# A token product split into full matmuls and 64-row tiles, moved into another burst and other banks, with the additions behind the squares

## The chip, the cores and the metric

The kernel runs on one core of a Trainium2 chip. The metric is the device time of one execution in microseconds. Each kernel was run several times, together with the kernel before on the same chip; a profile of one execution of each is read alongside. The engines' names in the profile: PE is TensorE (PEld its weight loads), ACT is ScalarE, DVE is VectorE, POOL is GpSimd, and SP is SyncE, which here only issues DMAs. The granted clock is the share of TensorE's full clock that the profile's records show.

## The reference, cut to what matters

```python
scores = scale * np.matmul(q, k.transpose(0, 1, 3, 2))       # 8 batches, 12 heads, 448 tokens, width 64
attn = np.maximum(scores, 0.0) ** 2 / S
x = (attn @ v)                                               # put together to (8, 448, 768)
h = np.maximum(xt @ w_tok1, 0.0) @ w_tok2                    # xt: tokens last; 448 -> 256 -> 448
u = x + h.transpose(0, 2, 1)                                 # the residual addition
out = u + np.maximum(u @ w_ch1, 0.0) @ w_ch2                 # 768 -> 1536 -> 768
```

The product over tokens has a sum of 448 terms: three blocks of 128 tokens and one of 64. That last block of 64 is what the change is about.

## The kernel before

Work is cut into 24 groups of four heads. Step i of the main loop does the scores of group i, and the values, the transposition, the two token products and the residual addition of group i - 1. Between them stand units of the channel products of earlier batches, taken from a queue by `fill`: a unit of the first channel product is 6 matmuls, one of the second is 12. They are ballast that keeps TensorE busy while other engines work.

```python
def values(i, cs):                       # 7 x 4 tiles of 64x64, two banks, r = bank
    ...
        accs[i] = [ps_acc.tile([128, 512], FP32, tag=f"acc{r}", name="acc_ps") for r in range(2)]
    ...

def values_out(i, split=False):          # VectorE: bank r -> xT, scaled, 448 of 512 columns; the rest is zero
    ...

def token1(i):                           # full matmuls, the fourth block half zeros
    x_sb = x_tiles.pop(i)
    ps = ps_mm.tile([128, JC, 256], FP32, tag="bank", name="t1_ps")
    for j in range(JC):
        for c in range(4):
            nc.tensor.matmul(ps[:, j, :], lhsT=wt1[:, c, j * 128 : (j + 1) * 128],
                             rhs=x_sb[:, :, c, :], start=(c == 0), stop=(c == 3))
    r1 = mix.tile([128, JC, 256], BF16, name="r1_sb")
    nc.scalar.activation(r1, ps, AF.Relu)

def token2(i, ...):                      # h: 4 matmuls into acc0, acc1; then one VectorE addition per bank
    ...

for i in range(DB + 1, ND + 2):          # DB = 3, ND = 24, XDMA = 8
    ...
    scores(i, 0); scores(i, 1)
    values(i - 1, range(QC)); values_out(i - 1)
    scores(i, 2)
    ...
    x_back(i - 1)                        # from step 9 on a transposing DMA: xT -> x_sb
    ...
    square()                             # VectorE squares what scores left
    if i - 1 >= XDMA:
        fill(1 / 3)
    scores(i, 3); scores(i, 4)
    transposes(i + 1)                    # into acc0, acc1
    square()
    if not slow:                         # slow: steps up to 6
        fill(2 / 9)
    token1(i - 1)
    fill(1 / 3 if slow else 1 / 9, least=1)
    scores(i, 5); scores(i, 6)
    token2(i - 1)
    ...
    square()
    fill(1 / 3, least=1 if slow else 0)
```

(Written shorter: lines joined, conditions at the loop's ends cut.) The two banks named acc0 and acc1 go round: values, transposes, h, values again.

## Time and profile before

| | before |
|---|---|
| time, median of 6 runs | 377.62 us (377.41 to 378.09) |
| span of the profile | 375.6 us |
| PE busy | 365.1 us, 97% |
| DVE, ACT busy | 208.1 us (55%), 211.4 us (56%) |
| PE waits named by the profile, together | some 6 us, of which 5 in the first 40 us |

How to read it: busy shares of the engines beside PE say nothing as long as what they deliver comes before PE asks for it. So the question at each spot is which arrives last: the turn of a matmul in PE's stream, or the bank and the data that it needs.

Two lines of groups show the token product before. Columns: line, engine, operation, out<-in, shapes, count, then busy us, mean ns of one, and the idle time ahead with what ended it.

```profile
L261 PE MATMUL t_ps<-x_sb,wt 128*128 128x256 bf16 x192 | 24.9, 273 | 1.8 <-DMA x_sb<-xT 0.8 <-DVE qkT L156 0.5 <-DVE x_sb L252 0.5
...
L269 ACT ACTIVATE r_sb<-t_ps 128x512 bf16<-128x512 f32 x24 | 14.3, 597 | 20.8 <-PE t_ps L261 20.8
```

Eight matmuls and one activation per group of heads. The 0.8 us wait is the one in step 9.

### The profile page before, as it was taken

What the parts mean: (1) busy time and instruction counts of PE and PEld (TensorE: products, weight loads), DVE (VectorE), ACT (ScalarE), POOL (GpSimd) and SP (SyncE); (2) the same over time, 40 slices, a digit from 0 to 9 for tenths busy, and PEclk for the clock granted to TensorE, in tenths of its full rate; (3) what the DMA queues carried; (4) which work ended last, traced back from release to release, by engine and by line L of the source; (5) the groups of instructions that cost most, each with busy time, mean ns of one, the idle gap of its engine ahead of it and who ended that gap; (6) DMA issues with size and microseconds to landing.
All of it is one profiled execution on the core that took longest, in us unless ns stands there. A gap on an engine that the chain in (4) does not pass through costs nothing.

```text
span 375.6 us, 10084 instructions
## 1 busy us (share of the span) xinstructions
PE 365.1 (97%) x4335; PEld 200.8 (53%) x4335; DVE 208.1 (55%) x376; ACT 211.4 (56%) x295; POOL 100.7 (27%) x186
## 2 busy tenths in 40 slices
PE   8889999999999999999999999999999999999995
PEld 3444555555555555565555555555555654555563
DVE  2896688675567665466555575465555664221021
ACT  4887888777434457744675447754576346412400
POOL 8874548313230321430321303312300000000000
PEclk9999999999999999999999999999999999999999
DMA  8999999934987876756844897838550443433023
GB/s 153 112 142 203 173 205 185 191 46 70 133 155 171 164 148 110 91 94 129 151 71 65 148 151 125 125 62 159 111 95 12 92 101 85 58 70 86 0 62 107
DMA packets 69325, 43.30 MB, mean 115 GB/s; under 512 B 43360, under 2 KB 65824, under 8 KB 69280
## 3 DMA queue, kind: packets, MB, share of 16 engines
q0 software_dynamic: 24416, 21.47, 40.4%
q1 hardware_dynamic: 44560, 20.75, 25.3%
q8 instruction: 34, 0.56, 0.6%
q10 hardware_dynamic: 304, 0.43, 0.4%
q14 instruction: 11, 0.09, 0.1%
HBM read 43.38 MB, written 11.01 MB: 145 GB/s over the span
## 4 chain that ended last, share of the span: by engine, by line
PE 90%; DVE 5%; ACT 2%; DMA 1%; issue 0%; ACTq 0%
PE m_ps L335 29%; PE m_ps L374 29%; PE sc_ps L166 9%; PE acc_ps L199 8%; PE t_ps L261 5%; PE h_ps L284 5%; PE qkT_ps L142 2%; DVE at L187 2%; ACT at L180 2%; DMA x_sb<-xT 1%; PE warm_ps L437 1%; DVE uT_sb L294 1%; DVE qkT L156 1%; PE x_ps L243 1%; PE m_ps L353 1%; DVE x_sb L252 1%
## 5 line engine op out<-in xcount | busy, mean ns | idle before, releaser
L180 ACT ACTIVATE at<-sc_ps 128x896 bf16<-128x896 f32 x167 | 143.9, 921 | 59.2 <-PE sc_ps L166 59.2
L335 PE MATMUL m_ps<-uT_sb,wc 128*128 128x448 bf16 x564 | 115.6, 353 | 0.2 <-DVE uT_sb L294 0.2
L374 PE MATMUL m_ps<-wc,r_sb 128*128 128x384 bf16 x672 | 115.2, 326 | 0.0
L187 DVE TENSOR_TENSOR at<-at 128x896 bf16<-128x896 bf16 x168 | 97.6, 624 | 4.6 <-ACT at L180 4.6
L374 PEld LDWEIGHTS <-r_sb 128*128 128x128 bf16 x672 | 64.3, 98 | 45.6 <-issue 3.9
L342 ACT ACTIVATE r_sb<-m_ps 128x448 bf16<-128x448 f32 x94 | 51.2, 544 | 59.8 <-PE m_ps L335 59.5
L335 PEld LDWEIGHTS <-wc 128*128 128x128 bf16 x564 | 53.3, 98 | 49.8 <-issue 4.3
L381 DVE TENSOR_TENSOR out_sb<-m_ps,u_sb 128x384 f32<-128x384 f32 x56 | 31.1, 556 | 60.3 <-PE m_ps L374 59.3
L166 PE MATMUL sc_ps<-qkT 64*64 64x448 bf16 x672 | 52.8, 360 | 0.9 <-ACT at L180 0.5
L294 DVE TENSOR_TENSOR uT_sb<-h_ps,xT 128x448 bf16<-128x448 f32 x48 | 27.9, 620 | 38.7 <-PE h_ps L284 38.6
L217 DVE TENSOR_SCALAR xT<-acc_ps 128x448 bf16<-128x448 f32 x45 | 26.1, 620 | 34.8 <-PE acc_ps L199 34.8
L199 PE MATMUL acc_ps<-at,v_raw 64*64 64x448 bf16 x672 | 38.4, 350 | 0.6 <-ACT x_sb L252 0.5
L556 POOL COPY gate<-x_sb 1x1 bf16<-1x1 bf16 x12 | 2.2, 184 | 125.5 <-DMA x_sb<-xT 125.5
L83 POOL DMA_DIRECT2D q_raw<-in_q_dram x48 | 29.0, 615 | 20.4 <-DMA wc<-in_moe_w_ch_dram 16.5
L156 DVE COPY qkT<-qkT_ps 128x896 bf16<-128x896 bf16 x45 | 26.0, 619 | 14.6 <-PE qkT_ps L142 14.6
L83 POOL DMA_DIRECT2D v_raw<-in_v_dram x48 | 29.5, 639 | 7.6 <-DMA wc<-in_moe_w_ch_dram 4.7
L166 PEld LDWEIGHTS <-qkT 64*64 64x64 bf16 x672 | 15.6, 105 | 28.1 <-issue 23.8
L83 POOL DMA_DIRECT2D k_raw<-in_k_dram x46 | 28.1, 633 | 0.0
L199 PEld LDWEIGHTS <-v_raw 64*64 64x64 bf16 x672 | 20.3, 107 | 13.1 <-issue 1.7
L261 PE MATMUL t_ps<-x_sb,wt 128*128 128x256 bf16 x192 | 24.9, 273 | 1.8 <-DMA x_sb<-xT 0.8
L269 ACT ACTIVATE r_sb<-t_ps 128x512 bf16<-128x512 f32 x24 | 14.3, 597 | 20.8 <-PE t_ps L261 20.8
L284 PE MATMUL h_ps<-wt,r_sb 128*128 128x448 bf16 x96 | 22.5, 355 | 0.0
(41 smaller groups left out, 119.8 us busy)
## 6 DMA issues: line engine op xcount, KB each, us to landing
out_dram<-out_sb SPq DMA_DIRECT2D x54, 192.0 KB, 3.5
q_raw<-in_q_dram POOLq DMA_DIRECT2D x48, 112.0 KB, 4.3
v_raw<-in_v_dram POOLq DMA_DIRECT2D x48, 112.0 KB, 5.6
k_raw<-in_k_dram POOLq DMA_DIRECT2D x46, 112.0 KB, 5.7
wc<-in_moe_w_ch_dram POOLq DMA_DIRECT2D x4, 1152.0 KB, 10.7
u_sb<-uT_sb SPq DMA_TRANSPOSE x48, 2.6
x_sb<-xT SPq DMA_TRANSPOSE x16, 3.3
k_first<-in_k_dram SPq DMA_DIRECT2D x1, 224.0 KB, 3.5
```

The lines of the kernel that those rows point to most:

```text
L83: eng.dma_start(out=dst[64 * r : 64 * (r + 1)].rearrange("p g c d -> p g (c d)"), in_=src[b, h0 : h0 + 2].rearrange("g (p c) d -> p g (c d ...
L166: nc.tensor.matmul(ps[64 * r : 64 * (r + 1), g, :S], lhsT=sb[h, r, 1, c * 64 : (c + 1) * 64], rhs=sb[h, r, 0, :], start=True, stop=True, s ...
L180: nc.scalar.activation(at, ps[:, :, :S], AF.Relu)
L187: nc.vector.tensor_tensor(out=at, in0=at, in1=at, op=ALU.mult)
L199: nc.tensor.matmul(ps[r][64 * g : 64 * (g + 1), :S], lhsT=v_raw[h, g, c, :], rhs=at[h, g, :], start=(c == 0), stop=(c == QC - 1), skip_gro ...
L261: nc.tensor.matmul(ps[:, j, :], lhsT=wt1[:, c, j * 128 : (j + 1) * 128], rhs=x_sb[:, :, c, :], start=(c == 0), stop=(c == 3),)
L284: nc.tensor.matmul(parts[r][:, :S], lhsT=r1[:, j, r * 128 : (r + 1) * 128], rhs=wt2[:, j, :], start=(j == 0), stop=(j == JC - 1),)
L294: nc.vector.tensor_tensor(out=uT_tiles[b // 2][:, 2 * d + r, off : off + S], in0=parts[r][:, :S], in1=xT[b % 2][:, 2 * d + r, :S], op=ALU.add,
L335: nc.tensor.matmul(ps[:, :S], lhsT=wc1[:, g, e * 128 : (e + 1) * 128], rhs=uT[:, g, off : off + S], start=(g == 0), stop=(g == CC - 1),)
L342: nc.scalar.activation(r2[:, e, off : off + S], ps[:, :S], AF.Relu)
L374: nc.tensor.matmul(ps[:, :HN], lhsT=r2[:, e, t * 128 : (t + 1) * 128], rhs=wc2[:, e, cols], start=(e == 0), stop=(e == EC - 1),)
L381: nc.vector.tensor_tensor(out=o[:, cols].rearrange("n (g d) -> n g d", d=128), in0=ps[:, :HN].rearrange("n (g d) -> n g d", d=128), in1=u_ ...
```

## The change

Its intent: of the eight token matmuls, the two with the last 64 tokens use half the rows of the array for zeros. Now the last 64 tokens are written twice, side by side, so that after the transposition they lie on both row halves; the two row halves then work for the two output blocks (j) at once, as four tiles of 64 rows by 64 columns. They stand directly ahead of scores 5 and 6, which also are 64-row tiles, so that the tiling need not be changed for them alone; and the product goes into acc0 and acc1, one row half to each bank. Some fill goes ahead of it, and one unit now stands between scores 6 and h. Squares go ahead of the residual additions from step 7 on. In step 0 four warm-up matmuls go.

```diff
-            fill(1 / 3)
+            fill(0.37, least=1)
         ... scores 3, 4, transposes, square
-        if not slow:
-            fill(2 / 9)
-        if 0 <= i - 1 < ND:
-            token1(i - 1)
-        fill(1 / 3 if slow else 1 / 9, least=1)
+        if slow:
+            token1(i - 1)
+            fill(1 / 3, least=1)
+        else:
+            fill(0.37, least=1)
+            if back:
+                token1_main(i - 1)          # 2 x 3 full matmuls into acc0, acc1
         if i < ND:
+            if not slow:
+                token1_rest(i - 1)          # 4 tiles, then one activation per bank
             scores(i, 5)
             scores(i, 6)
+        if not slow:
+            square()
+            fill(0.1, least=1)
         token2(i - 1)
         ...
         square()
-        fill(1 / 3, least=1 if slow else 0)
+        fill(1 / 3 if slow else 0.16, least=1)
```

```diff
+    def token1_rest(i):
+        for m in range(2):
+            cols = slice(64 * m, 64 * (m + 1))
+            for j in range(JC):
+                h = slice(64 * j, 64 * (j + 1))
+                nc.tensor.matmul(ps[j][cols, :256], lhsT=wt1_last[h, cols] if j else wt1[h, 3, cols],
+                                 rhs=x_sb[h, :, 3, :], start=False, stop=True, ...)
+        for j in range(JC):
+            nc.scalar.activation(r1[:, j, :], ps[j][:, :256], AF.Relu)
     def values_out(...):
+        if i > 2 * DB - 1:
+            for r in range(2):              # two more VectorE copies, 128x64
+                nc.vector.tensor_scalar(out=xT[b % 2][:, 2 * d + r, S:], in0=ps[r][:, S - 64 : S], ...)
-                keep_clock(0 if c == 3 else 1 if c > 4 else 2, warm_ps)
+                keep_clock(0 if c in (3, 4) else 1 if c > 4 else 2, warm_ps)
```

More of the change, by code (lines that the diff above doesn't have):

```diff
@@ L63 @@
     wt1 = wpool.tile([128, 4, DT], BF16, name="wt1")
+    wt1_last = wpool.tile([128, 128], BF16, name="wt1_last")
     wt2_nat = wpool.tile([128, JC, S], BF16, name="wt2_nat")
@@ L96, in load_wt1, with load_wt1_last @@
             nc.gpsimd.dma_start(out=wt1[r : r + 64, c // 2, :], in_=w[c])
+    def load_wt1_last():
+        w = moe_w_tok1.rearrange("(p c) j -> c p j", c=QC)
+        nc.gpsimd.dma_start(out=wt1_last[64:], in_=w[QC - 1, :, DT - 128 :])
     def load_wt2():
@@ L223, in values_out @@
             )
-    x_tiles, r1_tiles, uT_tiles = {}, {}, {}
+        if i > 2 * DB - 1:
+            for r in range(2):
+                nc.vector.tensor_scalar(
+                    out=xT[b % 2][:, 2 * d + r, S:],
+                    in0=ps[r][:, S - 64 : S],
+                    scalar1=float(alpha2),
+                    scalar2=None,
+                    op0=ALU.mult,
+                )
+    x_tiles, t1s, r1_tiles, uT_tiles = {}, {}, {}, {}
     XDMA = 8
@@ L269, in token1, with token1_main @@
         nc.scalar.activation(r1, ps, AF.Relu)
+        r1_tiles[i] = r1
+    def token1_main(i):
+        x_sb = x_tiles[i]
+        t1s[i] = ps = [
+            ps_acc.tile([128, 512], FP32, tag=f"acc{j}", name="t1_ps2") for j in range(JC)
+        ]
+        for j in range(JC):
+            for c in range(3):
+                nc.tensor.matmul(
+                    ps[j][:, :256],
+                    lhsT=wt1[:, c, j * 128 : (j + 1) * 128],
+                    rhs=x_sb[:, :, c, :],
+                    start=(c == 0),
+                    stop=False,
+                    skip_group_check=True,
+                )
+    def token1_rest(i):
+        x_sb, ps = x_tiles.pop(i), t1s.pop(i)
+        for m in range(2):
+            cols = slice(64 * m, 64 * (m + 1))
+            for j in range(JC):
+                h = slice(64 * j, 64 * (j + 1))
+                nc.tensor.matmul(
+                    ps[j][cols, :256],
+                    lhsT=wt1_last[h, cols] if j else wt1[h, 3, cols],
+                    rhs=x_sb[h, :, 3, :],
+                    start=False,
+                    stop=True,
+                    skip_group_check=True,
+                )
+        r1 = mix.tile([128, JC, 256], BF16, name="r1_sb")
+        for j in range(JC):
+            nc.scalar.activation(r1[:, j, :], ps[j][:, :256], AF.Relu)
         r1_tiles[i] = r1
@@ L534 @@
         slow = i <= 2 * DB
+        back = i - 1 < ND
         if i == 2 * DB + 1:
@@ L559 @@
             load_wc2(1, 2)
+            load_wt1_last()
         square()
         if i - 1 >= XDMA:
-            fill(1 / 3)
+            fill(0.37, least=1)
         if i < ND:
@@ L568 @@
         square()
-        if not slow:
-            fill(2 / 9)
-        if 0 <= i - 1 < ND:
+        if slow:
             token1(i - 1)
-        fill(1 / 3 if slow else 1 / 9, least=1)
+            fill(1 / 3, least=1)
[3 more added lines that the diff above has]
+                token1_main(i - 1)
         if i < ND:
+            if not slow:
+                token1_rest(i - 1)
             scores(i, 5)
             scores(i, 6)
-        if 0 <= i - 1 < ND:
+        elif back:
+            token1_rest(i - 1)
+        if not slow:
+            square()
+            fill(0.1, least=1)
+        if back:
             token2(i - 1)
@@ L580 @@
                 channel_work((i - 1) // DB)
-            if i == 2 * DB + 1:
-                hold_back(0, uT_tiles[1][:1, 0, :1])
-                for _ in range(DB):
-                    u_back(u_later.pop(0))
+        if i == 2 * DB + 1:
+            hold_back(0, uT_tiles[1][:1, 0, :1])
+            for _ in range(DB):
+                u_back(u_later.pop(0))
         square()
-        fill(1 / 3, least=1 if slow else 0)
+        fill(1 / 3 if slow else 0.16, least=1)
     while queue:
```

## The prediction

> **What bounds the kernel now.** I read the busy shares first, then the chain that ended last, the waits of TensorE, and the timeline of two steps.
>
> ```profile
> PE 365.1 (97%) x4335; PEld 200.8 (53%) x4335; DVE 208.1 (55%) x376; ACT 211.4 (56%) x295; POOL 100.7 (27%) x186
> ...
> PE 90%; DVE 5%; ACT 2%; DMA 1%; issue 0%; ACTq 0%
> ```
>
> TensorE (PE) is busy for 97% of the 375.6 us span and carries 90% of the chain; VectorE and ScalarE are near half. From about 39 us on, PE runs as one unbroken stream. Its waits are few, and only two of them touch the change:
>
> ```profile
> PE warm_ps L444 <- DVE qkT L156: 1.2, 1, 1.2
> ...
> PE t_ps L261 <- DMA x_sb<-xT: 0.8, 1, 0.8
> ```
>
> So a saving must be PE time taken out of the stream, or one of these two waits; and the risk is a new PE wait.
>
> A step of the loop has three bursts in 64-row tiles (scores 0, 1, values, score 2; scores 3, 4 and transposes; scores 5, 6), with 128-row work between them. This is the end of one such step and the start of the next, where the fill is the first channel product:
>
> ```profile
> 150.44 2.44 PE L335 MATMUL m_ps<-uT_sb,wc 128*128 128x448 bf16 x12
> ...
> 152.72 1.04 PE L261 MATMUL t_ps<-x_sb,wt 128*128 128x256 bf16 x8
> 153.59 1.30 PE L335 MATMUL m_ps<-uT_sb,wc 128*128 128x448 bf16 x6
> ...
> 154.82 0.57 PE L166 MATMUL sc_ps<-qkT 64*64 64x448 bf16 x8
> ...
> 155.32 0.93 PE L284 MATMUL h_ps<-wt,r_sb 128*128 128x448 bf16 x4
> 155.37 1.72 ACT L180 ACTIVATE at<-sc_ps 128x896 bf16<-128x896 f32 x2
> 155.91 1.16 DVE L294 TENSOR_TENSOR uT_sb<-h_ps,xT 128x448 bf16<-128x448 f32 x2 [3.13 <-PE h_ps L284]
> 156.09 2.43 PE L335 MATMUL m_ps<-uT_sb,wc 128*128 128x448 bf16 x12
> 156.99 1.15 DVE L187 TENSOR_TENSOR at<-at 128x896 bf16<-128x896 bf16 x2
> ...
> 158.45 0.57 PE L166 MATMUL sc_ps<-qkT 64*64 64x448 bf16 x8
> ...
> 158.86 1.49 PE L199 MATMUL acc_ps<-at,v_raw 64*64 64x448 bf16 x28
> ```
>
> The first column is the start, the second the duration. I take differences of starts, because groups overlap: the eight token matmuls take 152.72 to 153.59 = 0.87 us (0.90 in steps whose fill is the second product). The reader should also see the slack before: the residual additions end at 155.91 + 1.16 = 157.07, and the values, which need the same banks, begin at 158.86, 1.8 us later.
>
> **What the Trainium skill says.** "Perfetto Trace Analysis", Tensor Engine Instruction: the reported end of a matmul is an estimate; the rows agree, since 12 matmuls "last" 2.44 us and the next starts after 2.28, which is why I use starts. "TensorE: Matmul & The Clock Gate", Back-to-back issue gap: N/2.4 + 2.5 ns when warm, 109 ns for N = 256; eight in 0.87 to 0.90 us are 109 to 112 ns each, so this agrees. "TensorEngine Tiling (Array Packing)", Key Properties: changing the tiling mode drains TensorE. The trace agrees: the two scores take 0.40 us when another 64-row group follows (158.45 to 158.86) and 0.50 when a 128-row one does, and six channel matmuls take 1.14 us inside the stream (half of 2.28) but 1.23 ahead of scores (153.59 to 154.82). A round trip is 0.10 + 0.09 = about 0.19 us. Same page, Gotcha 1: different row tiles must not use one PSUM bank at the same time; the two row halves here go to different banks, and no run shows more yet.
>
> **The change part by part.** The instruction order of both programs shows steps 7 to 24 altered (18 steps), and one spot in step 0.
>
> (a) Token product. Six full matmuls and four 64-row tiles replace eight full ones. Six cost 6 x 0.109 = 0.65 us. The four tiles lie in four quadrants; the values run 28 such tiles of 448 columns in 158.86 to 160.18 = 1.32 us, 0.19 per four, so tiles work side by side at full rate and four of 256 columns cost about 0.11 to 0.12. 0.88 - 0.65 - 0.12 = 0.11 us less a step, 18 x 0.11 = 2.0 us. The tiles stand directly ahead of scores 5, 6, so no mode change is added, except in step 24, which has no scores and pays 0.19 more. Net **-1.8 us**, all on the path.
>
> (b) The DMA wait. In step 9 the token product waits 0.82 us for its transposed input (PE free at 107.75, start at 108.57). The new order puts two second-product units between transposes and token product instead of one, 1.96 us more PE work there. Even if the input comes 0.3 us later (see d), the wait is covered: **-0.8 us**.
>
> (c) Start. Four warm-up matmuls go from ahead of score 5 in step 0. They waited 1.22 us for a bank; now score 5 goes ahead of the wait. But the first h product at 23.05 needs a weight that GpSimd finishes reordering at 20.75 + 2.14 = 22.89 us, after its own load. This floor lets little through: **-0.1 us** (my choice; 0 to 0.5).
>
> (d) Added side work. VectorE gets two 128x64 copies a step. The 128x448 copy takes 0.62 us; at one element a cycle, 64 columns come to about 0.22, started 0.16 apart: 0.3 us a step, 6 us in all on an engine 55% busy. ScalarE gets two 128x256 activations for one of 128x512 (0.60 us). From 0.54 for 448 and 0.92 for 896 columns the slope is 0.85 ns per column, so 0.38 each, some 0.17 us more a step, 3 us in all. Both are hidden, save through (e). The extra weight load is one small DMA.
>
> (e) A new wait. This is the part that can eat the gain. In steps filled with first-product units the new order is: tiles, scores 5, 6, one unit, h, one unit, scores, values. From the start of scores 5 as zero: ScalarE starts the two token activations at about 0.20 and the two scores' at 0.74, ending 2.47. Squares now go first: they run 1.70 to 2.32 and 2.51 to 3.13. The residual additions, 1.16 us for the pair, then end at 4.25. PE: scores to 0.50, unit to 1.65, h to 2.42, unit to 3.63, scores to 4.04, values from 4.04. The values need both banks, free at about 4.30: **a wait of some 0.26 us** where there were 1.8 us of slack. The order shows this pattern in steps 7, 11, 12, 14, 17, 18 and 20, and in step 23 without the scores between, where it would be 0.67. Sum 7 x 0.26 + 0.67 = 2.5 us. With second-product units (1.96 us each) the values start at 5.7 and nothing waits. The sum rests on a chain of six estimated handovers, and 0.2 us of error in them clears most of it, so I count half: **+1.3 us**.
>
> Sum: -1.8 - 0.8 - 0.1 + 1.3 = -1.4; 377.7 - 1.4 = **376.3 us**.
>
> **The rivals.** First, the new wait in full: 377.5 us, no gain. For it: the handover times above are measured for their kinds. Against: six additions in a row, and an author who chose this order of squares and additions for the late steps alone. Second, no new wait: 375.0 us, or 374.6 if the start gives its half microsecond. For it: PE is otherwise bound by its own work. Third, the transposed input becomes the wait: the transposes land after 3.3 us (median), start 0.3 us later, and in steps 11, 17 and 23 less fill lies ahead of the token product (one second-product and two first-product units). In 11 and 17 the input is there 6.4 us after the start of the values and wanted at 6.9; in 23, which has no transposes, wanted at 6.4. So 0 to 0.2 us once, up to 1 us if loads crowd the queues as in step 9, where landing took 4.9. Fourth, VectorE or ScalarE as the bound: at 55 and 56% plus about 2 points they are not. Fifth, the clock falls because warm-ups went: the wait in step 0 is no longer than before, so I expect the granted clock to stay near 0.998.
>
> **Range and chances.** The corners are 374.6 and 377.5, with a run spread of 0.3 us, and up to 0.5 us for the third rival: 374.4 to 377.9 holds it 8 times in 10. 2% is 7.5 us, more than anything named here, so within 2% is nearly sure.
>
> **What would show it.** (a) Starts from the first token matmul to scores 5 of about 0.77 us, and PE busy about 2 us lower. (b) No PE wait on the transposed input in step 9. (c) First h product still near 22.9 us. (d) VectorE +6 us, ScalarE +3 us busy, no more on the chain. (e) PE waits of the values on the residual addition, 0.2 to 0.3 us in seven steps and one of 0.6 to 0.7 near the end; if absent, the result lies near 375.0. The prediction fails if a matmul in the new tiles costs more than a quarter of a group (a drain between the two modes on the same banks), if the start lets through over 0.5 us, or if a PE wait shows that I haven't named.

## The result, and the profile after

The changed kernel takes 378.68 us (median of 6 runs, 377.72 to 379.64), the kernel before 377.62 us in the same rounds. The ratio is 1.0027 with a 95% interval of 1.0009 to 1.0045: a little slower, about 1.0 us. Ratios here are the mean time of one kernel's fast runs over that of the other's of the same rounds, so not quite the ratio of the medians. All runs were fast (none was over 1.5% above the fastest of its kernel), at a granted clock of 0.997 to 1.0.

The page of the changed kernel, busy shares and the chain that ended last:

```profile
PE 364.3 (97%) x4367; PEld 200.6 (53%) x4367; DVE 212.8 (57%) x412; ACT 211.6 (56%) x313; POOL 100.7 (27%) x187
...
PE 87%; DVE 6%; ACT 3%; DMA 2%; issue 1%; SPq 0%; ACTq 0%; DVEq 0%
```

VectorE has 36 instructions more and 4.7 us more to do, ScalarE hardly more. PE is only 0.8 us less busy, although the tiles and the warm-ups that went should have taken more than twice that; and 3% of the chain have gone from PE to other engines. So something on PE's path waits, and a part of the wait is counted as busy. The list of waits of PE after:

```profile
PE t_ps L294 <- DMA x_sb<-xT: 1.0, 1, 1.0
PE qkT_ps L148 <- ACT k_raw L89: 0.9, 1, 0.9
PE warm_ps L495 <- DVE qkT L162: 0.7, 1, 0.7
...
PE acc_ps L205 <- DVE uT_sb L345: 0.2, 1, 0.2
```

The wait of the warm-ups fell from 1.2 to 0.7; the wait on the transposed input did not vanish but is 1.0; the values (acc_ps) wait for the residual addition (uT_sb) only once, for 0.2 us, as far as this list knows. The timeline of a step whose fill is the first channel product tells more (start, duration, then as before):

```profile
153.17 0.82 PE L294 MATMUL t_ps<-x_sb,wt 128*128 128x256 bf16 x6
...
153.92 0.29 PE L310 MATMUL t_ps<-x_sb,wt 64*64 64x256 bf16 x1
...
154.05 0.55 PE L172 MATMUL sc_ps<-qkT 64*64 64x448 bf16 x8
154.33 0.66 ACT L320 ACTIVATE r_sb<-t_ps 128x256 bf16<-128x256 f32 x2 [0.41 <-PE t_ps L310]
...
154.87 1.74 ACT L186 ACTIVATE at<-sc_ps 128x896 bf16<-128x896 f32 x2
155.68 0.92 PE L335 MATMUL h_ps<-wt,r_sb 128*128 128x448 bf16 x4
155.83 0.62 DVE L193 TENSOR_TENSOR at<-at 128x896 bf16<-128x896 bf16 x1 [3.73 <-ACT at L186]
...
156.64 0.62 DVE L193 TENSOR_TENSOR at<-at 128x896 bf16<-128x896 bf16 x1 [0.18 <-ACT at L186]
157.18 1.15 DVE L345 TENSOR_TENSOR uT_sb<-h_ps,xT 128x448 bf16<-128x448 f32 x2
157.66 0.57 PE L172 MATMUL sc_ps<-qkT 64*64 64x448 bf16 x8
...
158.07 1.82 PE L205 MATMUL acc_ps<-at,v_raw 64*64 64x448 bf16 x28
...
159.55 0.54 PE L172 MATMUL sc_ps<-qkT 64*64 64x448 bf16 x4
160.01 4.07 PE L425 MATMUL m_ps<-wc,r_sb 128*128 128x384 bf16 x24
```

Read it from the scores at 154.05. The additions start when the second square ends, and end at 157.18 + 1.15 = 158.33, 4.28 us after the scores. The values start at 158.07, on time, and no idle time is reported. But the group takes 1.82 us instead of 1.49, the score behind it comes 1.48 us after its start instead of 1.32, and the channel product 0.46 after that instead of 0.29. Together 0.16 + 0.17 = **0.33 us lost**, without a wait in any list: the first pair of tiles works on acc0, which is free at 157.18 + 0.62 = 157.80, while the second pair has to wait for acc1 until 158.33. By the starts of the single matmuls it begins at 158.38, 0.31 us after the first, and the next pair on acc0, which stands behind it in the program, begins with it. From then on the two row halves run one chunk out of step, and the group ends 0.33 us later. The same 1.82 or 1.83 us stands behind steps 7, 11, 12, 14, 17, 18 and 20 (the values are the first work of the step after); the other groups of the late steps take 1.49, but for the last: behind step 23 the values come with no scores ahead of them and start in two parts, 0.53 us apart, and there the timeline labels 0.15 us as a wait on the addition. Compared with the run that has additions first (second experiment below), this last group costs 0.71 us.

### The profile page after: what moved, and what is told of

It reads as the page before. It is cut to its first block, busy times and chain, and to the rows that moved or that the text cites. A ratio compares the mean times of both kernels' runs of the same rounds, so it can differ in the third digit from the quotient of the medians.

```text
span 375.9 us, 10212 instructions
## 1 busy us (share of the span) xinstructions
PE 364.3 (97%) x4367; PEld 200.6 (53%) x4367; DVE 212.8 (57%) x412; ACT 211.6 (56%) x313; POOL 100.7 (27%) x187
## 4 chain that ended last, share of the span: by engine, by line
PE 87%; DVE 6%; ACT 3%; DMA 2%; issue 1%; SPq 0%; ACTq 0%; DVEq 0%
PE m_ps L425 29%; PE m_ps L386 28%; PE acc_ps L205 9%; PE sc_ps L172 8%; PE h_ps L335 4%; PE t_ps L294 3%; PE qkT_ps L148 3%; DVE at L193 2%; ACT at L186 2%; DMA x_sb<-xT 1%; DVE uT_sb L345 1%; PE t_ps L310 1%; DMA k_first<-in_k_dram 1%; PE t_ps L276 1%; DVE qkT L162 1%; PE x_ps L258 1%
## 5 line engine op out<-in xcount | busy, mean ns | idle before, releaser
L193 DVE TENSOR_TENSOR at<-at 128x896 bf16<-128x896 bf16 x168 | 99.0, 625 | 52.2 <-ACT at L186 52.0
L386 PEld LDWEIGHTS <-wc 128*128 128x128 bf16 x564 | 52.4, 98 | 53.2 <-issue 7.9
L172 PE MATMUL sc_ps<-qkT 64*64 64x448 bf16 x672 | 54.1, 358 | 1.0 <-ACT at L186 0.6
L205 PE MATMUL acc_ps<-at,v_raw 64*64 64x448 bf16 x672 | 41.0, 351 | 0.9 <-ACT x_sb L267 0.5
L320 ACT ACTIVATE r_sb<-t_ps 128x256 bf16<-128x256 f32 x36 | 11.8, 381 | 31.7 <-PE t_ps L310 27.6
L205 PEld LDWEIGHTS <-v_raw 64*64 64x64 bf16 x672 | 21.8, 106 | 14.6 <-issue 4.9
L172 PEld LDWEIGHTS <-qkT 64*64 64x64 bf16 x672 | 17.5, 105 | 21.6 <-issue 17.7
L294 PE MATMUL t_ps<-x_sb,wt 128*128 128x256 bf16 x108 | 14.7, 273 | 1.0 <-DMA x_sb<-xT 1.0
```

The source lines that it names most:

```text
L172: nc.tensor.matmul(ps[64 * r : 64 * (r + 1), g, :S], lhsT=sb[h, r, 1, c * 64 : (c + 1) * 64], rhs=sb[h, r, 0, :], start=True, stop=True, s ...
L193: nc.vector.tensor_tensor(out=at, in0=at, in1=at, op=ALU.mult)
L205: nc.tensor.matmul(ps[r][64 * g : 64 * (g + 1), :S], lhsT=v_raw[h, g, c, :], rhs=at[h, g, :], start=(c == 0), stop=(c == QC - 1), skip_gro ...
L386: nc.tensor.matmul(ps[:, :S], lhsT=wc1[:, g, e * 128 : (e + 1) * 128], rhs=uT[:, g, off : off + S], start=(g == 0), stop=(g == CC - 1),)
```

## The experiments

Seven kernels were run. In the first call the kernel before had a median of 377.86 us (11 runs), in the second, on another chip, 378.15 us (9 runs); for this reason ratios are given too. The last three kernels of the table are of the second call. All gave correct results.

| kernel | median us | ratio to before | 95% interval |
|---|---|---|---|
| changed, again | 378.56 | 1.0020 | 1.0008 to 1.0032 |
| changed, additions first | 375.49 | 0.9933 | 0.9921 to 0.9945 |
| before, without the four warm-ups | 377.17 | 0.9984 | 0.9970 to 0.9997 |
| changed, eight full matmuls, no tiles | 377.41 | 0.9990 | 0.9977 to 1.0003 |
| changed, second bank's addition first | 378.89 | 1.0024 | 1.0006 to 1.0043 |
| full matmuls and additions first | 377.40 | 0.9981 | 0.9967 to 0.9994 |
| additions first and fill moved | 374.38 | 0.9904 | 0.9890 to 0.9917 |

My theory, A: the values wait for the second residual addition because squares go first. The rivals: B, the transposed input comes late where little fill is ahead of it; C, the tiles cost what they save.

### The changed kernel once more

No edit.

> The changed kernel once more, unaltered. Theory A (the values wait for the second residual addition in eight late steps): again 378.2 to 379.0 us, and in the profile the values group of the seven steps filled with first-product units has a duration of 1.83 us instead of 1.49, and the next score starts 1.48 us after it instead of 1.32; the extra is the same in every run. Theory B (the transposed input of the token product comes late in the steps with little fill ahead of it): the same time, but the runs differ from each other by over a microsecond, and the profile shows a wait on that transfer of another length than 1.0 us, or in another of the steps 11, 17, 23. Both may hold.

Measured: 378.56 us, range 378.18 to 379.07, ratio 1.0020. The values groups of 1.83 us stand behind the same seven steps, and the wait on the transposed input is again 1.0 us, again in step 11. So both effects are there in both profiles of this kernel, at the same places; they are not an accident of one execution. The runs' range decides nothing on the scatter that theory B asked for: it is 0.9 us here, was 1.9 us in the first set of this kernel, and is 1.1 us for the kernel before. One thing is new: in this execution the first h product waited 0.5 us for the reordered weight.

```profile
PE h_ps L335 <- POOL wt L111: 0.5, 1, 0.5
```

### Additions first

```diff
         if not slow:
-            square()
             fill(0.1, least=1)
```

> The changed kernel with one edit: the squares of scores 5 and 6 go back behind the residual additions in the late steps. Theory A: the additions end at about 3.4 us after the start of scores 5 instead of 4.28, the values need the banks at 4.02, so the wait is gone: 7 x 0.33 + 0.65 = 3.0 us less, 375.7 us, and all values groups take 1.49 us. Theory B alone: no change, 378.7 us. A third possibility, that the order was chosen because late squares hold up the values: 0 to 1 us slower, with PE waits of the values on the squares.

Measured: 375.49 us, ratio 0.9933: 3.1 us less than the changed kernel, by the medians of one call. The timeline of the same step:

```profile
153.95 0.55 PE L172 MATMUL sc_ps<-qkT 64*64 64x448 bf16 x8
...
156.16 1.16 DVE L345 TENSOR_TENSOR uT_sb<-h_ps,xT 128x448 bf16<-128x448 f32 x2 [4.16 <-PE h_ps L335]
...
157.23 1.15 DVE L193 TENSOR_TENSOR at<-at 128x896 bf16<-128x896 bf16 x2
...
157.96 1.49 PE L205 MATMUL acc_ps<-at,v_raw 64*64 64x448 bf16 x28
```

The additions now end 3.37 us after the scores, 0.64 us ahead of the values, and every group of values takes 1.49 us or, once, 1.52. The squares end at 158.38, and the values get as far as the chunks that need them about a microsecond after 157.96: nothing waits for them. Theory A holds with its size; the third possibility named there is out.

### The warm-ups alone

```diff
-                keep_clock(0 if c == 3 else 1 if c > 4 else 2, warm_ps)
+                keep_clock(0 if c in (3, 4) else 1 if c > 4 else 2, warm_ps)
```

This is made on the kernel before.

> The kernel before with only the four warm-up matmuls of score 4 in step 0 taken away. From the two profiles (second product of scores' step at 38.46 instead of 39.32 us, although the first key block came 0.2 us later): 0.9 to 1.1 us faster than before, 376.6 us. The prediction's floor (the reordered weight of the first h product) would allow 0.1 us, 377.5 us.

Measured: 377.17 us against 377.86, ratio 0.9984, so 0.6 us less with an interval of 0.1 to 1.1. That is less than the 0.9 to 1.1 expected from one pair of profiles and more than the prediction's 0.1. The start depends on when the first loads land, and these differ from execution to execution: in this profile TensorE also waited 0.4 us for the first query block. The granted clock was 0.998, so these four warm-ups were not needed for it.

### Eight full matmuls in the new place

```diff
-            for c in range(3):
+            for c in range(4):
...
-        for m in range(2):          # in token1_rest: no tiles
+        for m in range(0):
```

> The changed kernel with eight full token matmuls in the same place and banks, no 64-row tiles. If the tiles save what the prediction worked out, 0.11 us in each of 18 steps less 0.19 in step 24, this is 1.8 us slower than the changed kernel, some 380.4 us. If the switch of tiling between the six matmuls and the four tiles costs what they save, there is no difference. PE starts from the first token matmul to scores 5 should be about 0.98 us (0.90 plus the switch) against 0.875.

Measured: 377.41 us, ratio 0.9990. This refutes what I expected: without the tiles the kernel is 1.15 us faster, not 1.8 slower. Before taking this for theory C, look at the same step:

```profile
152.97 1.04 PE L294 MATMUL t_ps<-x_sb,wt 128*128 128x256 bf16 x8
...
153.67 0.76 ACT L320 ACTIVATE r_sb<-t_ps 128x256 bf16<-128x256 f32 x2
153.94 0.57 PE L172 MATMUL sc_ps<-qkT 64*64 64x448 bf16 x8
154.37 1.73 ACT L186 ACTIVATE at<-sc_ps 128x896 bf16<-128x896 f32 x2
...
156.68 1.15 DVE L345 TENSOR_TENSOR uT_sb<-h_ps,xT 128x448 bf16<-128x448 f32 x2
...
157.98 1.49 PE L205 MATMUL acc_ps<-at,v_raw 64*64 64x448 bf16 x28
```

The token product takes 0.97 us up to the scores, against 0.88 with tiles, as expected. But the first bank is complete after four matmuls, and its activation starts at 153.67, ahead of the scores; with tiles both banks are complete only at the end, and it starts 0.28 us after the scores' start. So ScalarE comes to the scores after 0.43 us instead of 0.82, squares and additions move up by as much, and the additions end 3.89 us after the scores' start. The values come at 4.04: no wait, apart from the last group, behind step 23, which takes 1.81 us. (The wait on the transposed input was 0.6 us in this profile instead of 1.0, which can be a part of the 1.15.) The full matmuls gain what the wait cost and pay what the tiles saved. The two effects have to be taken apart, which the sixth kernel does.

### The second bank's addition first

```diff
-        for r in rs:
+        for r in (rs if between or early else rs[::-1]):
```

> The changed kernel with the two residual additions of a late step in the other order, the second bank's first. If the lost 0.33 us in each of seven steps is the values' second pair of tiles waiting for its bank (hidden in the durations of the group, as the first pair starts on time), then now the first pair waits too: the time stays within 0.5 us of the changed kernel's 378.6, all values groups go back to 1.49 us, and the list of waits shows PE waiting for the residual addition for some 7 x 0.33 + 0.6 = 2.9 us in 8 places instead of 0.2 in one. If the loss is something else (slower tiles after the new ones, say), the 1.83 us groups stay and no wait appears.

Measured: 378.89 us, within 0.3 us of the changed kernel. No group of 1.83 us is left; they take 1.52 where they took 1.83. In the step shown above the scores start at 158.27 and the values at 158.99, 0.72 us later instead of 0.40: nearly the whole 0.33 us now stands ahead of the group, as the theory says.

```profile
157.79 1.15 DVE L345 TENSOR_TENSOR uT_sb<-h_ps,xT 128x448 bf16<-128x448 f32 x2
158.27 0.57 PE L172 MATMUL sc_ps<-qkT 64*64 64x448 bf16 x8
...
158.99 1.52 PE L205 MATMUL acc_ps<-at,v_raw 64*64 64x448 bf16 x28
```

In all eight groups the first values matmul starts 0.05 us after the reported end of the last addition; in the changed kernel the second pair did so. The list of waits, however, gives only 0.6 us in one place, not the 2.9 us expected in eight. The trace has the other seven waits too, each ended by the addition, but as gaps of 0.14 to 0.15 us: the scores' reported durations reach over the end of their work (0.57 us, where the next tiles can follow after 0.40) and cover the rest, and the list names only gaps of more than 0.15 us. That part of the expectation was wrong, and it is a warning: a missing entry in the list of waits doesn't prove that nothing waited. (The other order also costs a little elsewhere: the channel product at 69 us waits 0.5 us for its addition instead of 0.2.)

### Full matmuls, additions first

This has the edits of the second and the fourth kernel.

> Eight full token matmuls (no tiles) and residual additions first. With full tiles the squares-first order cost only in step 23 (values of 1.81 us there, 1.49 elsewhere), because the token activation of the first bank starts 0.4 us before scores 5; so the tiles' own saving was masked. Against the changed kernel with additions first (375.5 us) this run shows it alone: 18 x 0.11 - 0.19 = 1.8 us slower, less 0.4 for the shorter wait on the transposed input (0.6 instead of 1.0), so 376.9 to 377.3 us. If the tiles save nothing, 375.5 us.

Measured: 377.40 us, ratio 0.9981, against 375.49 and 0.9933 with tiles. The tiles alone save 1.9 us by the medians, 1.8 by the ratios (0.0048 of 378). The wait on the input was 0.9 us here, not 0.6, so it hardly differs from the 1.0 with tiles. The comparison has a smaller blemish: in this profile the token product also came 0.1 us late in step 14 and 0.3 us late in step 17 (with tiles 0.1 us, in step 14 alone). The traces confirm the size without such steps: from values to values a step takes 0.11 us less with tiles (14.42 against 14.52 us, or 17.04 against 17.15), and step 24, which pays the change of tiling, 0.11 us more (0.98 against 0.87 us for its token product): 17 x 0.11 - 0.11 = 1.8 us. Theory C is out: the tiles save what was worked out for them.

### Fill moved to the steps with the late input

```diff
-            fill(0.37, least=1)
+            fill(0.37, least=2 if i % 6 == 5 else 1)      # both fills ahead of the token product
```

This is made on the kernel with additions first. In steps 11, 17 and 23 one unit of six matmuls more stands ahead of the token product, and one less in the step after.

> Additions first, and in steps 11, 17 and 23 one more first-product unit ahead of the token product (taken from the step after). If the 1.0 us wait on the transposed input in step 11 is the only thing lost to that transfer, it disappears: 374.5 us against 375.5, and no PE wait on the input is left. If the transfer is late because PE came earlier and something it depends on moves with it, the wait moves to another step and the time stays at 375.5.

Measured: 374.38 us, ratio 0.9904: 1.1 us less than with additions first alone, and no wait on the transposed input is left in its list. (It has a wait of 1.0 us on a value block that landed late, at 20 us, in the start; that is in this profile alone.) This is the fastest of all: its ratio to the kernel before is 0.9904, and that of the changed kernel 1.0020, so it is 1.0% ahead of the one and 1.2% of the other.

Where the 1.0 us came from can be seen in the changed kernel: SP issued the transposing DMA of step 11 at 133.39, and TensorE got to work at 138.41, 5.0 us later.

```profile
133.39 1.23 SPq L249 DMA_TRANSPOSE x_sb<-xT  x1
...
138.41 0.83 PE L294 MATMUL t_ps<-x_sb,wt 128*128 128x256 bf16 x6 [1.01 <-DMA x_sb<-xT]
```

In most steps the transfer takes about 3.35 us from its issue to the start of a GpSimd copy that waits for it, in others 4 to 5.5. With 3.35 it would have been in time in step 11. In the last kernel it took 3.38 us there, so that run had the fill to cover a late transfer and also no late transfer; which of the two removed the wait, this run does not tell. Why some transfers are late isn't settled. I lined up the packets of all DMAs with the instructions in all nine profiles (to about half a microsecond): of 38 such transfers over 4 us, 36 had a fetch of instructions by DMA under way within 3 us after their issue, of 70 shorter ones 25. Loads of queries, keys and values in flight show no such link. Stores of the output do, as strongly: SP had issued one within 5 us before 34 of the 38 late transfers, and before 21 of the 70 shorter ones. With both, 32 of 42 transfers were late, with the fetch alone 4 of 19, with the store alone 2 of 13, with neither 0 of 34. These are associations, found after the fact, and not a cause shown; no run here moves a fetch or a store alone.

## Why the prediction was wrong

The measured 378.68 us lies above the range of 374.4 to 377.9. Step by step, in the order of its own parts:

- **(a) The tiles, -1.8 us: right.** 1.8 to 1.9 us, from the sixth kernel against the second. In the timeline, first token matmul to scores 5 take 0.88 us: 0.65 for six matmuls, 0.10 for the change of tiling, 0.13 for the four tiles. My check "about 0.77" forgot that the change of tiling (counted at the scores before) now falls inside this stretch; the sum had it right.
- **(b) The DMA wait, -0.8 us: wrong by a microsecond.** Step 9 lost its wait, although its transfer took 5.4 us this time. But in step 11, where the new order leaves less fill ahead of the token product, 1.0 us came up in its place. The term that failed is the time to landing in step 11: 3.3 us was assumed, 5.0 us measured. The third rival named this step and this size, "up to 1 us if loads crowd the queues" (the loads that it blamed show no link, see above), and the sum left it out. Net +0.2.
- **(c) The start, -0.1 us: too small.** 0.6 us (0.1 to 1.1). The floor that I saw, the reordered weight of the first h product, is real: three of the seven experiments' profiles show TensorE waiting 0.5 us for it. But I took the end of the whole reordering, two copies of 1.1 us, as one fixed time. It varies by two microseconds from execution to execution, from 21.2 to 23.2 us in the nine profiles, and in the profile of the changed kernel it was 22.24. And only the second matmul of that product needs the second copy: here the first started at 22.18, before the copy's end, and the second at 22.38.
- **(d) The side work: hidden, as said; single sizes right, sums too large.** 36 copies of 0.214 us (0.22 said), activations of 0.381 us (0.38 said). VectorE got +4.7 us rather than 6: a pair of copies takes 0.34 us, but in the profile it begins 0.09 us before the end of the copy ahead of it. ScalarE got +0.2 us rather than 3: the two activations overlap and take 0.66 us together, against 0.60 for the one before, so they add 0.06 us a step and not 0.17. None of it bound by itself.
- **(e) The new wait, +1.3 us: this is the step that failed.** The chain was right, within 0.1 us at every handover and within 0.03 at its ends: additions ending at 4.25 us (4.28 measured), values at 4.04 (4.02), the steps 7, 11, 12, 14, 17, 18, 20 and one more at the end. I had worked out 2.5 us and then counted half, as "0.2 us of error in them clears most of it" and because an author had chosen the order. The runs show 3.1 us (378.56 against 375.49). It is more than 2.5 because a step loses 0.33 us, not 0.26: the second pair starts 0.05 us after the reported end of the addition, as assumed, but the additions end 0.03 us later and the values come 0.02 us earlier than worked out, so the pair is 0.31 us late, and the two row halves out of step add 0.02. With 0.71 for the last group (0.67 said) the profile gives 7 x 0.33 + 0.71 = 3.0 us. Neither reason for halving was a measurement.

The terms as measured: -1.8 + 0.2 - 0.6 + 3.1 = +0.9 us, against +1.0 us (first set of runs) and +0.7 (second set). So the parts account for the result, within the 0.5 us to either side that the interval of (c) leaves. The range was also narrower than the prediction's own terms: the wait in full (377.5), the third rival's 1 us and the spread of 0.3 us reach 378.8 us; the 377.9 written down holds hardly any of that rival. The check named for (e), "PE waits of the values on the residual addition, 0.2 to 0.3 us in seven steps", would have failed if taken literally: the list of waits has only one such entry. The loss had to be read from starts and durations.

What stays open is why the late transfers are late, which of fill and an early landing ended the wait in step 11, and whether the order with squares first was good in some other arrangement of fill. In this one it costs 3.1 us.

## What to carry to other kernels

When TensorE runs without gaps, work out for each bank when its last reader ends and when TensorE wants it again; a slack of 1.8 us can be used up by three small moves (later activation, squares ahead, one unit less in between) of which none looks dangerous alone. If such a count says that a wait arises, put it in at full size unless something measured speaks against it. And test a part of a change with its partner removed as well: here the tiles looked harmful (full matmuls 1.15 us faster) until the order of squares and additions was put right, and then saved 1.9 us.

## What the Trainium skill lacked or had wrong

- "TensorEngine Tiling (Array Packing)", Key Properties, says that a change of tiling mode drains TensorE, without a size. Here it costs 0.09 to 0.10 us each way (two scores 0.40 us ahead of tiles of the same mode, 0.50 us ahead of a 128-row group; six token matmuls 0.65 us by the spacing of 0.109 us, 0.75 us ahead of the tiles).
- "Perfetto Trace Analysis", Tensor Engine Instruction, says that the end of a matmul is estimated. It doesn't say what follows for waits: a pair of tiles held up for 0.31 us inside a group of 28 left no idle time at all in the profile, and of 3.1 us lost in a kernel 0.2 us stood in the list of waits.
- No page has a measured cost of one late bank of two for tiles in two row halves: the group of values lost 0.33 us to a bank that kept its pair waiting for 0.31 us, and about as much when the late bank was that of the first pair instead of the second (378.89 and 378.56 us).
- "DMA: Bandwidth & Descriptors", Latency and other measured facts, has no landing time for a small transposing DMA between places in SBUF. Here it is, from the issue to the start of the copy that waits, about 3.35 us in most cases and 4 to 5.5 in 38 of 108, 36 of these with an instruction fetch within 3 us after the issue and 34 with an output store issued within 5 us before it.
